# Another order for the instructions of a two-layer convolution and MLP kernel, with some loads issued earlier

## The chip, the cores and the metric

The kernel runs on one core of a Trainium2 chip. The core has five engines with their own instruction streams: TensorE (PE, matrix products into PSUM), VectorE (DVE), ScalarE (ACT), GpSimd (POOL) and SyncE (SP), which here only issues DMAs. The metric is the device time of one execution in microseconds; less is better.

## The reference

One sequence of S = 2048 positions and D = 512 channels passes twice through a pair of layers, in bfloat16. Layer A convolves k with four taps per channel, multiplies by v, convolves the product causally over the whole sequence with a filter of length 2048 per channel (by FFT of length 4096), adds a skip, and multiplies by the layer norm of x. Layer B is an MLP with 1376 hidden features behind two layer norms. Both are added to x.

```python
def _A_ref(q, k, v, shift_k, ssm_k, ssm_D):
    ...
    for t in range(ks):
        k_shift = k_shift + k_pad[:, t:t + S, :] * shift_k[:, ks - 1 - t][None, None, :]
    kv = k_shift * v
    ...
    y_f = kv_f * kf_f[None, :, :, :]
    ...
    y = y + kv * ssm_D[None, None, :]
    return q * y

def _B_ref(x, w1, b1, w2, b2):
    y = _layernorm(x, axis=-1)
    h = _gelu(jnp.einsum("bsd,df->bsf", y, w1) + b1)
    return jnp.einsum("bsf,fd->bsd", h, w2) + b2

x = A_q
x = x + _A_ref(_layernorm(x, axis=-1), A_k, A_v, A_shift_k, A_ssm_k, A_ssm_D)
x = x + _B_ref(_layernorm(x, axis=-1), B_w1, B_b1, B_w2, B_b2)
x = x + _A_ref(_layernorm(x, axis=-1), A_k, A_v, A_shift_k, A_ssm_k, A_ssm_D)
x = x + _B_ref(_layernorm(x, axis=-1), B_w1, B_b1, B_w2, B_b2)
```

Both layers A use the same k, v and filters, so the long convolution y is computed once and used twice.

## The kernel before

**Stages.** The sequence is cut into two halves of 1024 positions. A number at the end of a stage's name is the half. The long convolution is done with matrix products in place of an FFT:

- ht: the filter is transposed on PE (`turn`, L561) and evicted from PSUM to SBUF (L480 on ACT, L481 on DVE).
- fir: k is transposed (L610), the four taps are applied as matmuls (L635 in half 0, L663 in half 1), and DVE multiplies by v while it reads PSUM (L641, L672).
- h1 and x1 (`stage1`, L578): the first transform of the filter and of k·v, eight groups of 16 matmuls in each half, each group evicted as one tile of 128 x 1024.
- h2 and x2 (`stage2`, L590): the second transform, eight groups each. For h2_0 a `swap` follows: eight DMAs of 256 KB on SP's queue (L460, `ar<-ar`) that exchange the partitions of real and imaginary parts.
- Products with the swapped spectrum on DVE (L475): sixteen of 128 x 1024 in half 0; in half 1 eight large ones called p2 (128 x 2048), eight after x2_1, and eight sums, all 128 x 2048.
- i1 and i2: the inverse transforms (L695, L717).

Then come the token blocks, 13 of them, q0 to q12: half 0 takes the 8 tiles of 128 positions of each layer pair as blocks of 1, 1, 2, 2, 2 tiles and then 2, 2, 2, 2; half 1 as 4, 4 and 4, 4. A block does:

- statistics of x on DVE: L831 (BN_STATS) and L832 (BN_AGGR);
- three small steps from variance to scale and mean: L836, L838 (a power with exponent -0.5, always on POOL), and the scaled mean, one instruction on DVE (L843) or one for each tile on POOL (L846);
- the norm, on ACT (L856) or DVE (L857), times y plus x (L475, 128 x 512);
- the same statistics again for layer B (called z), its norm, and a transpose by DMA on SP (L900; for the first tiles on PE, L908);
- m1: 11 groups of matmuls with w1 (L920), each followed by the gelu on ACT (L925);
- m2: matmuls with w2 (L954), added to x on DVE (L958), and the store.

Blocks of half 0 run beside the transforms of half 1. Later, when the transforms are done, what is left is mostly m1 and m2.

**What sets the order.** The class `Prog` records 1187 operations, with the memory that each reads and writes. `arrange` then puts them in the order of a table of numbers, `SEQ`; each engine runs its own operations in that order. A second table, `ENGS`, is a string with one letter for each operation that may run on more than one engine (a: ACT, v: DVE, p: POOL), and a third, `BANKS`, gives each PSUM tile its bank. `sync` puts in the semaphore waits that this order needs. Nothing is reordered at run time: an engine whose next instruction waits, waits with all that is behind it. POOL waits for its own last instruction as well.

Loads of 256 KB and more are `paced`: one may not start before the one 99 places ahead of it has landed.

The main lines are these:

```python
self.seq = [self.ops[i] for i in self.SEQ]
...
o.eng = o.engs[0] if len(o.engs) == 1 else {"a": ACT, "v": DVE, "p": POOL}[next(choice)]
...
P.op((DVE, POOL), lambda e: e.tensor_scalar(v, v, m1, a1, ALU.mult, ALU.add), {DVE: 65.0, POOL: 195.0}, reads=[v], writes=[v])
P.op(POOL, lambda e: e.tensor_tensor(r, v, hf, ALU.pow), 420.0 + 149.0 * n, reads=[v, hf], writes=[r])
```

The numbers in such calls are the planner's costs in nanoseconds. With the order given by a table they have no effect on which instruction stands where.

Of the kernel before, what the change touches and what calls it, by code (L numbers as in the profile page):

```python
# [36 lines left out]
class Prog:  # L37
# [65 lines left out]
            "avvvvaappavvapvavavpvvava")  # L103
    BANKS = (
            "26624320240260660466027405640260464422140204626240406006442460424046462022442640460444626002206020640220"
            "04023022660051677767117660640311026376367637332542537030213654742352762454741476061377362300423726574027"
            "07315704314621527766215047034261015330227471565340011503350731745320154030276054756")

    def __init__(self, nc):
# [885 lines left out]
```

## Time and profile before

| | |
|---|---|
| median of 3 runs | 236.0 us (235.88 to 236.41) |
| the profiled execution | 235.91 us |
| its span in the trace | 234.0 us |
| granted clock of PE | 1.00 |
| PE busy | 222.7 us (95%) |
| DVE busy | 178.7 us (76%) |
| ACT busy | 164.5 us (70%) |
| POOL busy | 55.5 us (24%) |

All times are microseconds from the start of the span. A line of the timeline gives start, duration, engine, source line, operation, output tile and input tile with their sizes, the count of like instructions that follow each other, and in square brackets the idle time ahead of them with what ended it. `ar` is the one large SBUF tensor that holds everything in bfloat16, `sm` the small fp32 one for statistics, `ps` is PSUM. Neighbouring instructions overlap by about 0.1 us, so the distance of two starts is somewhat less than the duration shown. In the chain of waits a line gives start, duration, engine, tile and source line; "issue" is time in which the engine waited for nothing that the trace shows.

### The profile page before, as it was taken

To read this page: it belongs to the slowest core of one execution; us is meant where nothing else is said; L and a number is where in the kernel's file an instruction comes from. 1 tells how busy PE (TensorE), PEld (TensorE's weight loads), DVE (VectorE), ACT (ScalarE), POOL (GpSimd) and SP (SyncE) were. 2 spreads that over 40 slices of the span, in tenths; PEclk is the share of its full clock that TensorE was granted. 3 is DMA by queue.
4 is the path that set the end of the run, shared out by engine and by line. 5 is a ranking of instruction groups with operands and counts; after the bars stand their busy time and mean duration, and the time that the engine had idled before them with its cause. 6 is when DMAs were issued, how large, how long until landed. Compare 5 with 4: busy or idle time off the path is not lost.

```text
span 234.0 us, 6498 instructions
## 1 busy us (share of the span) xinstructions
PE 222.7 (95%) x2743; PEld 147.1 (63%) x2765; DVE 178.7 (76%) x362; ACT 164.5 (70%) x262; POOL 55.5 (24%) x113
## 2 busy tenths in 40 slices
PE   7989887999999999999999999999999999999995
PEld 3878776967868596677966576644444444444454
DVE  0699998999999999999999988781777569410222
ACT  2789999989968688999879986488058216802710
POOL 2270132006403405639303331204011120200000
PEclk9999999999999999999999999999999999999999
DMA  6999489928994360033500313401300130170202
GB/s 185 381 386 305 147 229 274 324 65 150 144 211 126 70 158 3 1 48 72 155 4 3 90 24 68 134 3 22 69 0 3 28 62 0 23 115 0 90 0 92
DMA packets 40106, 24.93 MB, mean 107 GB/s; under 512 B 23591, under 2 KB 33677, under 8 KB 40077
## 3 DMA queue, kind: packets, MB, share of 16 engines
q1 hardware_dynamic: 39778, 24.36, 39.7%
q8 instruction: 22, 0.36, 0.7%
q10 hardware_dynamic: 298, 0.16, 0.4%
q14 instruction: 8, 0.06, 0.1%
HBM read 13.23 MB, written 2.10 MB: 66 GB/s over the span
## 4 chain that ended last, share of the span: by engine, by line
PE 58%; DVE 24%; ACT 10%; issue 2%; POOL 2%; DMA 2%; SPq 0%; DVEq 0%
PE ps L920 23%; PE ps L954 23%; DVE ar L475 13%; ACT ar L480 9%; PE ps L695 4%; DVE sm L831 3%; PE ps L590 2%; DMA ar<-in_A_ssm_k_dram 2%; DVE ar L672 2%; DVE ar L958 2%; DVE ar L641 2%; PE ps L717 1%; POOL sm L836 1%; PE ps L578 1%; PE ps L635 1%
## 5 line engine op out<-in xcount | busy, mean ns | idle before, releaser
L925 ACT ACTIVATE ar<-ps,sm 128x256 bf16<-128x256 f32 (+5 forms) x143 | 65.7, 523 | 33.2 <-PE ps L920 32.9
L920 PE MATMUL ps<-ar 128*128 128x256 bf16 (+5 forms) x569 | 81.9, 297 | 0.4 <-ACT ar L480 0.2
L480 ACT ACTIVATE ar<-ps 128x1024 bf16<-128x1024 f32 (+3 forms) x77 | 71.1, 998 | 11.0 <-PE ps L578 3.4
L954 PE MATMUL ps<-ar 128*128 128x512 bf16 (+1 forms) x323 | 75.9, 379 | 1.5 <-issue 0.6
L920 PEld LDWEIGHTS ps<-ar 128*128 128x128 bf16 (+1 forms) x572 | 52.9, 100 | 27.5 <-ACT ar L480 1.1
L475 DVE TENSOR_TENSOR ar<-ar 128x512 bf16<-128x512 bf16 (+2 forms) x104 | 62.7, 646 | 1.5 <-ACT ar L480 0.8
L954 PEld LDWEIGHTS ps<-ar 128*128 128x128 bf16 (+1 forms) x341 | 32.4, 98 | 35.3 <-ACT ar L925 0.4
L958 DVE TENSOR_TENSOR ar<-ar,ps 128x512 bf16<-128x512 bf16 x31 | 20.8, 680 | 32.9 <-PE ps L954 32.9
L831 DVE BATCH_NORM_STATS2 sm<-ar 128x6 f32<-128x512 bf16 x64 | 42.5, 685 | 0.5
L856 ACT ACTIVATE ar<-ar,sm 128x512 bf16<-128x512 bf16 x39 | 30.6, 813 | 12.9 <-DVE sm L843 8.8
L836 POOL TENSOR_SCALAR sm<-sm 128x2 f32<-128x2 f32 (+2 forms) x22 | 9.9, 449 | 89.0 <-DVE sm L832 88.8
L838 POOL TENSOR_TENSOR sm<-sm 128x2 f32<-128x2 f32 (+2 forms) x26 | 21.7, 834 | 25.1 <-DVE sm L836 23.1
L590 PE MATMUL ps<-ar 128*128 128x64 bf16 x512 | 18.4, 193 | 1.5 <-DVE ar L481 0.7
L578 PE MATMUL ps<-ar 128*64 128x128 bf16 x512 | 17.9, 221 | 1.8 <-ACT ar L480 1.2
L590 PEld LDWEIGHTS ps<-ar 128*128 128x128 bf16 x512 | 16.8, 98 | 3.6 <-DVE ar L481 1.3
L578 PEld LDWEIGHTS ps<-ar 128*64 128x64 bf16 x512 | 14.9, 110 | 4.8 <-ACT ar L480 1.9
L481 DVE CAST ar<-ps 128x1024 bf16<-128x1024 f32 x12 | 14.6, 1218 | 1.2 <-PE ps L578 0.9
L846 POOL TENSOR_SCALAR sm<-sm 128x1 f32<-128x1 f32 x34 | 15.1, 460 | 1.6
L695 PE MATMUL ps<-ar 64*128 64x64 bf16 (+1 forms) x384 | 12.4, 203 | 1.0 <-DVE ar L475 0.9
L695 PEld LDWEIGHTS ps<-ar 64*128 64x128 bf16 (+1 forms) x384 | 11.8, 113 | 2.2 <-DVE ar L475 1.0
L857 DVE TENSOR_SCALAR ar<-ar,sm 128x512 bf16<-128x512 bf16 x25 | 10.3, 415 | 2.7 <-POOL sm L846 2.5
L788 DVE SCALAR_TENSOR_TENSOR ar<-ar,sm,ps 128x512 bf16<-128x512 bf16 x16 | 11.1, 740 | 0.3 <-PE ps L590 0.3
(45 smaller groups left out, 93.5 us busy)
## 6 DMA issues: line engine op xcount, KB each, us to landing
ar<-ar SPq DMA_DIRECT2D x16, 256.0 KB, 4.0
ar<-tab_s SPq DMA_DIRECT2D x9, 256.0 KB, 6.3
ar<-in_A_ssm_k_dram SPq DMA_DIRECT2D x8, 256.0 KB, 5.9
ar<-in_A_q_dram SPq DMA_DIRECT2D x8, 256.0 KB, 4.4
ar<-in_A_v_dram SPq DMA_DIRECT2D x8, 256.0 KB, 5.0
out_dram<-ar SPq DMA_DIRECT2D x7, 256.0 KB, 2.5
ar<-in_B_w_dram SPq DMA_DIRECT2D x4, 344.0 KB, 5.2
ar<-in_B_w_dram SPq DMA_DIRECT2D x5, 256.0 KB, 5.2
```

What stands on the lines that cost most here:

```text
L475: return P.op(eng, lambda e: e.tensor_tensor(o, a, b, op), dur, reads=[a, b] + list(more), writes=[o])
L480: return e.activation(dst, src(), AF.Copy)
L578: r = e.matmul(Q(tl, 64 * ri, 64, i * 128, [1, 128]), w, m, start=True, stop=True)
L590: r = e.matmul(Q(tl, 0, 128, i // 8 * 512 + i % 8 * 4, [32, 16], [1, 4]), w, m, start=True, stop=True)
L695: r = e.matmul(Q(tl, 0, 128, i, *([32, 16], [1, 4]) if split else ([1, 128],)), w, m, start=n == 0, stop=n == 1)
L831: P.op(DVE, lambda e, sj=sj, x=x: e.bn_stats(sj, x), 600.0, reads=[x], writes=[sj])
L838: P.op(POOL, lambda e: e.tensor_tensor(r, v, hf, ALU.pow), 420.0 + 149.0 * n, reads=[v, hf], writes=[r])
L856: return e.activation(o, x, AF.Identity, bias=u, scale=r)
L920: r = e.matmul(Q(tl, 0, rows, 0, [1, w]), a, m, start=dk == 0, stop=dk == 3)
L925: P.op(ACT, lambda e, dst=dst, tl=tl, rows=rows, bias=bias, w=w: e.activation(dst, Q(tl, 0, rows, 0, [1, w]), AF.Gelu_apprx_tanh, bias=bia ...
L954: r = e.matmul(Q(tl, 0, 128, 0, [1, 512]), ins[fc][0], ins[fc][1], start=fc == 0, stop=fc == 10)
L958: P.op(DVE, lambda e, x=x, tl=tl: e.tensor_tensor(x, x, Q(tl, 0, 128, 0, [1, 512]), ALU.add), 604.0, reads=[x], writes=[x], tile=tl)
```

## The change

Only the three tables change; the operations are the same 1187. The first 330 entries of `SEQ` come in another order, with loads of weights and of q at other places among them, and the rest is ordered anew. 40 operations run on another engine than before: 19 norms (eleven from ACT to DVE, eight from DVE to ACT), seven PSUM evictions, and otherwise small ones. ACT has 263 operations in place of 266, DVE 364 in place of 362, POOL 92 in place of 91; PE and SP have as many as before.

```diff
     SEQ = (
-        0, 46, 8, 45, 35, 2, 6, 3, 5, 36, 12, 9, 1, 10, 11, 25, 4, 44, 217, 7, 56, 197, 15, 50, 16, 57, 14, 13, 47,
...
+        2, 8, 45, 35, 0, 6, 36, 43, 3, 5, 44, 11, 9, 1, 10, 12, 4, 7, 25, 56, 197, 46, 216, 217, 15, 50, 57, 13, 16,
...
```

What the table moves is seen in the rows of each engine. A row is a source line, the operation, its output tile and input tile or the output's shape, and how many follow each other.

The first place is PE in the prologue, where the second transform of the filter (L590, h2_0) meets the first transform of k·v (L578, x1_0):

```order
 L590 MATMUL ps<-ar 128x16x4 x32
-L578 MATMUL ps<-ar 64x128 x32
-L590 MATMUL ps<-ar 128x16x4 x16
-L578 MATMUL ps<-ar 64x128 x32
-L590 MATMUL ps<-ar 128x16x4 x16
-L578 MATMUL ps<-ar 64x128 x16
+L578 MATMUL ps<-ar 64x128 x16
+L590 MATMUL ps<-ar 128x16x4 x16
+L578 MATMUL ps<-ar 64x128 x32
+L590 MATMUL ps<-ar 128x16x4 x16
+L578 MATMUL ps<-ar 64x128 x32
```

Each group of 16 is one tile. The two h2_0 groups now come after one and three groups of x1_0, where they came after two and four. SP, at the same stage, issues the eight swap DMAs (`ar<-ar`) with these loads between and behind them:

```order
 L460 DMA ar<-ar 64x8x256 x4
 L460 DMA ar<-in_B_w_dram 128x2x512
-L460 DMA ar<-ar 64x8x256 x4
+L460 DMA ar<-ar 64x8x256 x2
+L460 DMA ar<-in_B_w_dram 128x1376
+L460 DMA ar<-ar 64x8x256 x2
+L460 DMA ar<-in_B_w_dram 128x1376
+L460 DMA ar<-in_B_b_dram 128x10x1
+L460 DMA ar<-in_B_w_dram 128x1376
```

A piece of w1 (128x1376) stands between the last two pairs of swaps; another piece of w1 that stood ahead of the swaps is now behind them. Not shown: a piece of w2 (128x2x512) with the bias b2 has come from behind the swaps to ahead of the first.

The second place is ACT around x1_1, the first transform of half 1 (L480, 128x1024), and block q6, whose two norms are L856. Before:

```order
L480 ACTIVATE ar<-ps 128x1024 x2
L925 ACTIVATE ar<-ps,sm 128x256 x2
L480 ACTIVATE ar<-ps 128x1024
L925 ACTIVATE ar<-ps,sm 128x256
L480 ACTIVATE ar<-ps 128x1024
L856 ACTIVATE ar<-ar,sm 128x512
L480 ACTIVATE ar<-ps 128x1024 x3
L925 ACTIVATE ar<-ps,sm 128x256
L856 ACTIVATE ar<-ar,sm 128x512
```

And of the change:

```order
L480 ACTIVATE ar<-ps 128x1024 x2
L856 ACTIVATE ar<-ar,sm 128x512
L925 ACTIVATE ar<-ps,sm 128x256
L856 ACTIVATE ar<-ar,sm 128x512
L480 ACTIVATE ar<-ps 128x1024 x3
L925 ACTIVATE ar<-ps,sm 128x256
L480 ACTIVATE ar<-ps 128x1024 x2
L856 ACTIVATE ar<-ar,sm 128x512
L925 ACTIVATE ar<-ps,sm 128x256
```

Before, one norm of q6 (the first L856) stands behind four evictions; the other is on DVE. Now both are on ACT and stand behind two evictions. The last L856 of each piece belongs to the z statistic of block q5.

The third place is DVE around the last aggregate (L832) of q6, among the p2 products (L475, 128x32x64, the 128 x 2048 ones of the trace). Before, where the second L832 is that of q6:

```order
L475 TENSOR_TENSOR ar<-ar 128x32x64
L832 BN_AGGR sm<-sm 128x2
L475 TENSOR_TENSOR ar<-ar 128x32x64
L831 BN_STATS sm<-ar 128x6
L475 TENSOR_TENSOR ar<-ar 128x512
L832 BN_AGGR sm<-sm 128x2
L475 TENSOR_TENSOR ar<-ar 128x32x64 x3
L958 TENSOR_TENSOR ar<-ar,ps 128x512
L475 TENSOR_TENSOR ar<-ar 128x32x64
```

And of the change, where the first L832 is that of q6:

```order
L475 TENSOR_TENSOR ar<-ar 128x32x64
L832 BN_AGGR sm<-sm 128x2
L475 TENSOR_TENSOR ar<-ar 128x32x64
L475 TENSOR_TENSOR ar<-ar 128x512
L475 TENSOR_TENSOR ar<-ar 128x32x64
L831 BN_STATS sm<-ar 128x6
L475 TENSOR_TENSOR ar<-ar 128x32x64 x3
L831 BN_STATS sm<-ar 128x6
```

The aggregate has moved up: five large products are behind it now where four were.

More of the change, by code (lines that the diff above doesn't have):

```diff
@@ L44 @@
     SEQ = (
[55 rows of a table removed]
[55 rows of a table added]
     ENGS = (
-            "pvavvvvvavpvpapapaaavaaaaavaavaavavvvppvvvaavvaaavaavvaaaaaaaaavaaaaavaaaavaaaaaaapppvaaaaaaaaaaaaaaaaaa"
-            "avaaaaaaaaapvapvvavpvppaappvvpvaavpaappaappaappaappaappavppvappaappaappvappaapvaapvavvavvvvvapvvvvvppvaa"
-            "avvvvaappavvapvavavpvvava")
+            "pvaavvvvaapvvapvpaaaaaavvavaavaavavvvppvpvaavvaaavaavvaaaaaaaaavaaaaavaaaavaaaaaaavpppaaaaaaaaaaaaaaaava"
+            "aaaaaaaaaaappvpvvappvppaappvvpvaappaappaappaappaappaappvappaappvappaappavppaappaapvavavvvvvavpvvvavpvaaa"
+            "apvvvvavvvvvvvvaavvpvvvva")
     BANKS = (
-            "26624320240260660466027405640260464422140204626240406006442460424046462022442640460444626002206020640220"
-            "04023022660051677767117660640311026376367637332542537030213654742352762454741476061377362300423726574027"
-            "07315704314621527766215047034261015330227471565340011503350731745320154030276054756")
+            "06644620240260460466027405640260460422120204620426406026440246202657402442442202402046620620262446022424"
+            "40045202760061271673611270720311476106045110176745457463524552047013405341600727657677006645241006432235"
+            "02011725663061347154745325226234547674263125476530423505220630623103453761310741074")
     def __init__(self, nc):
```

108 rows, old and new, of the table SEQ are left out of this document.

## Prediction, made before the changed kernel ran

> **What bounds the kernel now.** I read the page first for which engine is full in which slice, then windows by stage, then the chain of waits, then each engine's timeline where the chain changes hands.
>
> ```profile
> span 234.0 us, 6498 instructions
> PE   7989887999999999999999999999999999999995
> DVE  0699998999999999999999988781777569410222
> ```
>
> TensorE (PE) is full from about slice 9 (53 us) to the end; VectorE (DVE) is full from slice 3 to slice 22 (129 us). The profiled execution took 235.91 us, of which the span is 234.0; the median of the runs is 236.0, 0.1 above it. I sum against 235.91. The windows below give, after the bounds and the length of a stretch, the busy time of PE, PE's weight loads, DVE, ScalarE (ACT) and GpSimd (POOL), then clock, DMA share and GB/s.
>
> ```profile
> 6.50:41.30 34.80, 30.04 (x765) 26.48 (x764) 31.75 (x52) 31.90 (x35) 9.69 (x24) 1.00 0.89 285
> 41.30:70.00 28.70, 27.74 (x491) 22.10 (x498) 27.99 (x58) 25.30 (x47) 6.89 (x17) 1.00 0.82 178
> 70.00:121.00 51.00, 50.26 (x688) 37.95 (x681) 50.42 (x83) 45.44 (x83) 20.58 (x28) 1.00 0.30 74
> 130.50:231.70 101.20, 100.69 (x525) 51.52 (x532) 58.82 (x147) 51.74 (x89) 13.57 (x25) 1.00 0.20 46
> ```
>
> PE is idle for 4.8 us before 41.3, then 1.0, 0.7 and, over the last 101 us, 0.5. The clock is 1.00 everywhere. So two things can move the end: when PE's full stretch begins, and any new hole in it. The chain of waits (start, us, engine, output tile, line) shows the hand-overs:
>
> ```profile
> 27.26 1.10 issue
> 41.32 7.39 PE ps L695 x128
> ...
> 90.35 3.35 POOL sm L836
> 93.70 0.07 issue
> 93.77 0.71 POOL sm L838
> 94.49 0.09 issue
> 94.58 1.17 POOL sm L846 x2
> 95.77 0.81 ACT ar L856
> ...
> 108.48 12.51 DVE ar L475 x11
> ```
>
> The first hand-over is in the prologue: the chain goes from the last eviction of h2_0 through the swaps to inverse1 of half 0 (L695, 41.32). The second, at 90 us, is a statistic of block q6: three small POOL steps that here take 5.2 us, then the norm on ACT (L856). The third is DVE's run of products that releases inverse1 of half 1. PE's last matmul ends at 231.7, and what follows it (the last add and store, and what lies outside the span) is 4.2 us of the 235.91. None of those operations changes.
>
> **The prologue: the swaps go out sooner.** The instruction counts hardly move (40 operations change engine, none is added), so the terms are waits and order.
>
> ```profile
> 8.59 1.23 DVE L481 CAST ar<-ps 128x1024 bf16<-128x1024 f32 x1 [0.33 <-PE ps L578]
> 21.36 1.22 DVE L481 CAST ar<-ps 128x1024 bf16<-128x1024 f32 x1
> 24.92 1.21 DVE L481 CAST ar<-ps 128x1024 bf16<-128x1024 f32 x1
> 26.05 0.68 DVE L831 BATCH_NORM_STATS2 sm<-ar 128x6 f32<-128x512 bf16 x1
> 27.22 1.23 DVE L481 CAST ar<-ps 128x1024 bf16<-128x1024 f32 x1 [0.33 <-PE ps L590]
> ```
>
> The CAST at 27.22 is the last eviction of h2_0; the swaps' DMAs wait for it. In the new order two things happen on the way. From 8.59 to the first x1_0 CAST at 21.36 DVE has 11.9 us of work and 0.9 of waiting. Its new list there starts at about 8.14 (before the printed wait of 0.33 and what is left of the instruction ahead; an estimate) with a small product, has one CAST more (1.13, the distance from 24.92 to 26.05), a norm and a halo copy more, and a mask product and some small work less: net +0.66. With the waiting gone, that CAST comes at 8.14 + 12.56 = 20.7, 0.66 sooner. Then PE takes each of the last two h2_0 groups one x1_0 group sooner, so the CAST of h2_0 no longer waits for PE. Between the two CASTs lie 5.86 us before (0.33 of which is the printed wait, and 0.25 another one); the new list has the same four CASTs, one more AGGR of 0.1, and no reason for either wait: 4.8 to 5.3. The CAST moves from 27.22 to 25.5, by 1.7; with the upper figure by 1.2.
>
> ```profile
> 28.48 3.28 SPq L460 DMA_DIRECT2D ar<-ar  x4
> 31.80 0.64 SPq L460 DMA_DIRECT2D ar<-in_B_w_dram  x1
> 33.25 3.21 SPq L460 DMA_DIRECT2D ar<-ar  x4
> DMA to landing us min/median/max: 2.9/4.8/5.6
> 36.35 6.11 DVE L475 TENSOR_TENSOR ar<-ar 128x1024 bf16<-128x1024 bf16 x10 [0.82 <-ACT ar L480]
> ```
>
> SP issues eight swaps in two fours, from 28.48 and from 33.25, each about 0.8 apart and landing after 4.8 (median). DVE's products follow, and the first i1_0 matmul at 41.32 follows them. Moving the first four by 1.7 gives 26.8; the second four depend on later evictions and move by 1.3, to 31.95. A w1 piece of 344 KB now stands between the last two pairs on the queue; at the window's 285 GB/s it is 1.2 us of DMA time, and 0.8 of issue time by the spacing of the swaps. The products wait for swaps pairwise and DVE works through them without a gap, so I take it as mostly hidden: i1_0 starts at 39.8 in place of 41.32, **−1.5**. Bounds: −1.7 (all of the CAST) and −0.3 (the w1 piece delays the last pair by its whole 1.2).
>
> **The loads that go sooner.** The first w2 piece moves from the middle of the program to before the first swap; w1 pieces move a few places, three queries one or two. No wait on a load ends last before 60 us in the chain, other than ssm_k's at the very start, so sooner landings win nothing by themselves: 0. Their cost is the queue time above, in the range 0 to 1.2.
>
> **Carrying −1.5 forward.** DVE is full between 41 and 121 (78.4 busy of 79.7), so it stays 1.5 earlier, and PE with it, until something with its own clock comes. That is the q6 statistic.
>
> **The new wait at q6.** Its last aggregate and what follows it on each engine, before:
>
> ```profile
> 90.06 0.19 DVE L832 BATCH_NORM_AGGREGATE sm<-sm 128x2 f32<-128x6 f32 x1
> 90.16 3.48 DVE L475 TENSOR_TENSOR ar<-ar 128x2048 bf16<-128x2048 bf16 x3
> 90.49 1.94 ACT L480 ACTIVATE ar<-ps 128x1024 bf16<-128x1024 f32 x2 [0.63 <-PE ps L578]
> 97.81 0.50 POOL L846 TENSOR_SCALAR sm<-sm 128x1 f32<-128x1 f32 x2
> 96.49 2.83 ACT L480 ACTIVATE ar<-ps 128x1024 bf16<-128x1024 f32 x3
> 99.20 0.48 ACT L925 ACTIVATE ar<-ps,sm 128x256 bf16<-128x256 f32 x1
> 99.45 0.63 PE L590 MATMUL ps<-ar 128*128 128x64 bf16 x16
> 100.78 0.19 POOL L836 TENSOR_SCALAR sm<-sm 128x2 f32<-128x2 f32 x1 [2.48 <-DVE sm L832]
> 105.67 1.13 POOL L836 TENSOR_SCALAR sm<-sm 128x2 f32<-128x2 f32 x1 [2.75 <-DVE sm L832]
> 105.52 2.36 DVE L475 TENSOR_TENSOR ar<-ar 128x2048 bf16<-128x2048 bf16 x2
> 108.54 4.54 POOL L846 TENSOR_SCALAR sm<-sm 128x1 f32<-128x1 f32 x2
> 108.41 5.77 DVE L475 TENSOR_TENSOR ar<-ar 128x2048 bf16<-128x2048 bf16 x5
> ```
>
> POOL's L836 takes 0.19 at 100.78, where DVE runs statistics, but 3.34 at 90.35, until the third of three 128x2048 products is over (the chain's 3.35), and 1.13 beside the products at 105.52. The two L846 at 108.54 take 2.27 each, two products each. So beside a run of large products a POOL step here lasts one to three of them.
>
> After, the aggregate stands earlier in DVE's list: after 1.5 of upstream gain and 1.7 of DVE work that now lies behind it, it comes at 86.85. Behind it stand a large product, a small one, a large one (together 2.65, so to 89.6), one statistic of 0.6, three large products (to 93.6), one statistic. POOL's L836 waits out the first group and ends about 89.7; L838 (0.71) fits into the statistic and ends about 90.5; the two L846 meet the run of three. At 2.27 each they would outlast it, so they end with it: the means are ready at **X = 93.5**. Before, they were ready at 95.75.
>
> That is sooner, and yet worse, since ACT's order changed more. Before, both x1_1 evictions of 90.49, two more and three gelus stood ahead of the first L856, and the second norm of q6 was on DVE. After, both norms of q6 are on ACT, and only two evictions stand ahead of them. ACT is through with these at about 90.3 (92.4, where the pair above ends, less the 1.5 and less the 0.63 that it waited; an estimate) and then waits for X: 3.2 us. Behind the first norm (0.72 from its start at 95.77 to the next at 96.49) wait a gelu that a w2 group on PE needs (0.38 of the 0.48 above, the rest overlaps), the second norm, five more evictions of x1_1 (0.91 each by the three at 96.49) and one more gelu: 0.72 + 0.38 + 0.72 + 4.55 + 0.38 = 6.75 from X to the first L590 matmul of half 1, which needs all of x1_1: **100.25**, where before it is at 99.45. PE, which the upstream gain had brought 1.5 ahead, is idle for 0.8 + 1.5 = 2.3 us on the way, first ahead of the w2 group that the gelu feeds.
>
> **The sum.** From the first x2_1 group PE is full to its end: 231.67 − 99.45 = 132.2 before. I take the same after, since 100.7 of the last 101.2 us are matmuls that both have. 93.5 + 6.75 + 132.2 = 232.45, against 231.67: +0.8. So 235.91 + 0.8 = **236.7 us**. Moved work in the last 100 us (eleven norms from ACT to DVE, eight the other way, two means from DVE to POOL) lies beside PE with DVE 58% and ACT 51% busy; I put it at 0, with 0.4 either way for one late norm.
>
> **Rivals.**
>
> *The POOL steps are held by one product each.* The rows for it: 1.13 at 105.67 for one L836, though a second product came right behind. Against it: 3.34 at 90.35 and 2.27 twice at 108.54. Then L838 ends at 90.5, L846 twice at the ends of two products, 91.5 and 92.5: X = 92.5, the first x2_1 group at 99.25, PE's end at 231.45, time **235.7**. The Trainium skill, page "SBUF — State Buffer", section "Who interferes with whom", says that a VectorE instruction with two SBUF inputs holds the port it shares with GpSimd for the whole instruction and that whoever issues first gets it; read literally, POOL gets in when the running product ends. The 3.34 us at 90.35 speaks against that reading, the 1.13 at 105.67 for it.
>
> *POOL is through before the run of three, and the gain of the prologue survives (the other side).* Place: the statistic of 0.6 between the two groups of products, and the change from one product to the next. If L836 starts before the first large product (0.1 us after the aggregate, where at 90.35 it came 0.19 after the product's start), or L838 and both L846 get in around the statistic, then X is 91.3 or less. The point from which it decides is X = 91.3: there the first x2_1 group comes at 91.3 + 6.75 = 98.05, which is 1.4 before 99.45, and with the 1.5 of the prologue it can hardly come sooner. From there each us of X costs one us; below, the gain is kept: 235.91 − 1.4 = **234.5**. For it: with DVE idle or on statistics the three steps take 0.19, 0.71 and 0.25 twice, 1.3 together, and would end at 88.5. Against it: no POOL step in the rows above that began beside a large product ended before that product.
>
> *The swaps are not sooner.* The w1 piece between the last two pairs and the early w2 piece ahead of the first share 285 GB/s with the loads that run there; the DMA share is 0.89 in this window. If the last pair lands 1.2 us later than I have it, i1_0 starts at 41.0, q6 and X move by 1.2 too: 236.7 + 1.2 = **237.9**. For it: the 0.89. Against: swaps land 2.9 to 5.6 after issue with a w2 load already between the fours.
>
> That the change doesn't do what it says, that is, that the sooner loads move nothing, is part of all cases: no case gains by them.
>
> **How the numbers follow.** A difference of 0.2%, 0.47 us, is about what a measurement of this kernel can tell from no change; so same is 235.5 to 236.5. Forecast (own range 236.0 to 237.5): 0.44, of which 0.10 falls within 0.2% and 0.34 is slower. One product each (235.2 to 236.2): 0.20, of which 0.13 is same and 0.07 faster. Kept gain (234.1 to 235.3): 0.23, faster. Swaps not sooner (237.3 to 238.5): 0.13, slower but for 0.01. Faster 0.30, same 0.24, slower 0.46. The range leaves out the lower edge of the kept gain and the upper half of the last case: 234.3 to 238.0.
>
> **What would show it.** In the changed kernel: the last h2_0 CAST at 25.5 and the first i1_0 matmul at 39.8 (right) or after 41 (third rival). POOL's L846 of q6 ending at about 93.5, at 92.5, or before 91.3. ACT idle 3 us before an L856 near 90, released by POOL, and PE idle about 2.3 us in all around an L954 near 92, or neither. The first L590 of half 1 at 100.25. PE's end 132 us after it; if that distance differs by over 0.5, the tail's moved norms matter and my zero for them is wrong.

## The result, and the profile after

The changed kernel takes **238.43 us** (median of ten runs, 236.92 to 239.40) beside 236.22 for the kernel before on the same chip (ten runs, 235.45 to 236.76): a ratio of 1.0089, 95% interval 1.0062 to 1.0115. It is slower by 2.2 us by the medians and 2.1 by the ratio, where +0.8 was forecast; the time lies 0.4 above the range. The profiled execution took 239.05 us. Medians here count every run; a ratio leaves out the runs that took over 1.5% longer than the fastest of their kernel.

The prologue first. In the timeline of the changed kernel (columns as before), SP's queue with the swaps (`ar<-ar`), then DVE from the first CAST of x1_0 to the products, then PE:

```profile
29.95 2.77 SPq L460 DMA_DIRECT2D ar<-ar  x4
32.76 0.84 SPq L460 DMA_DIRECT2D ar<-in_B_w_dram  x1
35.40 1.28 SPq L460 DMA_DIRECT2D ar<-ar  x2
36.72 1.27 SPq L460 DMA_DIRECT2D ar<-in_B_w_dram  x1
38.03 1.28 SPq L460 DMA_DIRECT2D ar<-ar  x2
...
22.62 1.22 DVE L481 CAST ar<-ps 128x1024 bf16<-128x1024 f32 x1
28.70 1.22 DVE L481 CAST ar<-ps 128x1024 bf16<-128x1024 f32 x1 [0.17 <-PE ps L590]
44.10 3.70 DVE L475 TENSOR_TENSOR ar<-ar 128x1024 bf16<-128x1024 bf16 x6 [1.40 <-DMA ar<-ar]
...
23.88 1.09 PE L590 MATMUL ps<-ar 128*128 128x64 bf16 x32 [0.80 <-ACT ar L480]
42.82 3.79 PE L695 MATMUL ps<-ar 128*128 128x128 bf16 x64 [0.25 <-DVE ar L475]
47.95 3.74 PE L695 MATMUL ps<-ar 128*128 128x128 bf16 x64 [1.33 <-DVE ar L475]
```

The swaps go out 1.5 us later than before (29.95 for 28.48), not sooner; in three more executions of this kernel (k1 to k3 below) they begin at 28.38, 28.39 and 29.02. The last pair stands behind a w1 piece whose issue alone takes 1.27, and DVE, which never waited for a swap before, waits 1.40 for it. So i1_0 starts at 42.82 (before 41.32) and then breaks in two: its second half begins at 47.95, behind a hole of 1.33.

Now q6, on POOL and ACT, and the first x2_1 groups on PE:

```profile
91.20 1.07 POOL L836 TENSOR_SCALAR sm<-sm 128x2 f32<-128x2 f32 x1 [6.71 <-DVE sm L832]
93.22 0.83 POOL L846 TENSOR_SCALAR sm<-sm 128x1 f32<-128x1 f32 x2
93.18 1.94 ACT L480 ACTIVATE ar<-ps 128x1024 bf16<-128x1024 f32 x2
94.99 0.83 ACT L856 ACTIVATE ar<-ar,sm 128x512 bf16<-128x512 bf16 x1
102.13 1.61 PE L590 MATMUL ps<-ar 128*128 128x64 bf16 x48
```

The means are ready at 94.05 (93.22 + 0.83), and ACT reaches the norm only at 94.99, with no idle time in its row: in this execution the forecast wait is not there. So the loss of this run must lie ahead of 90 us. To see that in all runs, I cut the time at three marks: the start of the last i1_0 matmul, the first inverse1 matmul of half 1 (L695, called i1_1 below) and the end of PE's last matmul. The three lower rows are the same changed kernel profiled again (experiments k1 to k3).

| execution | us | i1_0 starts | last i1_0 | from there to i1_1 | i1_1 to PE's end | behind it |
|---|---|---|---|---|---|---|
| before | 235.91 | 41.32 | 48.48 | 72.96 | 110.23 | 4.24 |
| changed | 239.05 | 42.82 | 51.47 | 73.06 | 110.36 | 4.16 |
| k1 | 238.14 | 41.96 | 50.53 | 73.07 | 110.38 | 4.16 |
| k2 | 242.63 | 41.26 | 50.04 | 76.96 | 111.46 | 4.17 |
| k3 | 240.01 | 42.58 | 51.12 | 73.05 | 110.38 | 5.46 |

Three losses can be read off. The **prologue** is later by 1.6 to 3.0 us in all four. The **rest** takes the same time as before to 0.3 us, but in k2 it takes 4.0 more in the stretch with q6 and 1.2 more in the last one. And in k3 1.3 us come outside the span (240.01 − 236.9 = 3.1, otherwise 1.8), for a reason that no run shows. Without a wait in the rest the parts add up to 237.6 us where the last i1_0 matmul comes at 50.04 and to 239.1 where it comes at 51.47; by this estimate the prologue alone accounts for the median of 238.43, and seven of the ten timed runs lie between the two.

### The profile page after: what moved, and what is told of

Read it like the earlier page. It is cut to its first block, busy times and chain, and to the rows that moved or that the text cites. A ratio compares the mean times of both kernels' runs of the same rounds, so it can differ in the third digit from the quotient of the medians.

```text
span 237.3 us, 6490 instructions
## 1 busy us (share of the span) xinstructions
PE 224.4 (95%) x2742; PEld 148.1 (62%) x2765; DVE 180.8 (76%) x364; ACT 162.5 (69%) x259; POOL 48.5 (20%) x109
## 4 chain that ended last, share of the span: by engine, by line
PE 81%; ACT 6%; DMA 4%; DVE 3%; issue 2%; SPq 1%; POOL 1%; ACTq 0%; POOLq 0%
PE ps L920 32%; PE ps L954 31%; ACT ar L480 6%; PE ps L578 5%; PE ps L590 4%; PE ps L717 3%; DMA ar<-ar 2%; DMA ar<-tab_small 2%; PE ps L695 2%; PE ps L561 2%; DVE ar L475 1%; SPq L460 1%; PE ps L943 1%; POOL ar L548 1%; PE ps L663 1%
## 5 line engine op out<-in xcount | busy, mean ns | idle before, releaser
L480 ACT ACTIVATE ar<-ps 128x1024 bf16<-128x1024 f32 (+3 forms) x76 | 70.2, 1002 | 13.2 <-PE ps L561 5.2
L475 DVE TENSOR_TENSOR ar<-ar 128x512 bf16<-128x512 bf16 (+3 forms) x105 | 63.0, 636 | 2.4 <-DMA ar<-ar 1.4
L856 ACT ACTIVATE ar<-ar,sm 128x512 bf16<-128x512 bf16 x36 | 28.3, 814 | 2.7 <-POOL sm L846 1.7
L836 POOL TENSOR_SCALAR sm<-sm 128x2 f32<-128x2 f32 (+2 forms) x23 | 6.7, 290 | 96.0 <-DVE sm L832 95.6
L838 POOL TENSOR_TENSOR sm<-sm 128x2 f32<-128x2 f32 (+2 forms) x26 | 20.4, 784 | 25.5 <-DVE sm L836 23.6
L578 PE MATMUL ps<-ar 128*64 128x128 bf16 x512 | 19.4, 231 | 1.4 <-ACT ar L480 0.9
L590 PE MATMUL ps<-ar 128*128 128x64 bf16 x512 | 18.6, 194 | 1.7 <-ACT ar L480 1.6
L590 PEld LDWEIGHTS ps<-ar 128*128 128x128 bf16 x512 | 16.9, 98 | 3.7 <-ACT ar L480 1.5
L578 PEld LDWEIGHTS ps<-ar 128*64 128x64 bf16 x512 | 16.3, 117 | 4.5 <-ACT ar L480 1.9
L481 DVE CAST ar<-ps 128x1024 bf16<-128x1024 f32 x13 | 15.8, 1221 | 3.6 <-PE ps L578 2.3
L695 PE MATMUL ps<-ar 64*128 64x64 bf16 (+1 forms) x384 | 12.5, 203 | 1.7 <-DVE ar L475 1.6
L695 PEld LDWEIGHTS ps<-ar 64*128 64x128 bf16 (+1 forms) x384 | 11.9, 114 | 3.0 <-ACT ar L480 2.2
L846 POOL TENSOR_SCALAR sm<-sm 128x1 f32<-128x1 f32 x29 | 12.4, 442 | 1.6
L832 DVE BATCH_NORM_AGGREGATE sm<-sm 128x2 f32<-128x6 f32 x64 | 10.6, 173 | 0.7
```

What stands on the lines that cost most here:

```text
L475: return P.op(eng, lambda e: e.tensor_tensor(o, a, b, op), dur, reads=[a, b] + list(more), writes=[o])
L480: return e.activation(dst, src(), AF.Copy)
L578: r = e.matmul(Q(tl, 64 * ri, 64, i * 128, [1, 128]), w, m, start=True, stop=True)
L590: r = e.matmul(Q(tl, 0, 128, i // 8 * 512 + i % 8 * 4, [32, 16], [1, 4]), w, m, start=True, stop=True)
L695: r = e.matmul(Q(tl, 0, 128, i, *([32, 16], [1, 4]) if split else ([1, 128],)), w, m, start=n == 0, stop=n == 1)
L856: return e.activation(o, x, AF.Identity, bias=u, scale=r)
```

## Experiments

Ratios are to the kernel before on the same chip, with 95% intervals; 0.001 of a ratio is 0.24 us.

**Which half of the table costs.** d1 has the first 280 operations of the old order, with their engines and banks, and the rest of the new; d2 the reverse.

```diff
 d1: SEQ = old[:280] + new order of the other operations
 d2: SEQ = new[:280] + old order of the other operations
```

> The first 280 operations (up to about 50 us) as in the kernel before, the rest in the order, on the engines and in the banks of the changed kernel. Theories Loads and Compute: nothing is lost behind the prologue, 236.0 to 236.5, and from the end of i1_0 to the start of i1_1 there are 73.0 us as in both kernels. Theory q6: the rest of the order costs what I predicted for it without the gain of the prologue, 2.3 us: 238.0 to 238.5, and the stretch grows to 75.

> The first 280 operations as in the changed kernel, the rest as in the kernel before. Theories Loads and Compute: the whole loss stays, 237.8 to 238.8. Theory q6: 235 to 236.5, for the prologue alone would not lose.

d1: 237.06 us, ratio 1.0019 (0.9996 to 1.0043). d2: 237.51 us, 1.0058 (1.0037 to 1.0078). By the ratios the new prologue costs 1.4 us alone and the new rest 0.45, with an interval that reaches below 0; together 1.8 of the 2.1. d1's runs go from 235.60 to 242.62, and the slowest, the profiled one, has a hole of 2.17 us on PE at 97 us.

**The loads.** c1 is the changed kernel with the loads up to the last swap at their old places in the DMA queues, here shown around the swaps; c2 is the kernel before with the loads up to the last swap at their new places. The loads behind the swaps stay where each kernel has them.

```diff
 c1, SP around the swaps:
 L460 DMA ar<-ar 64x8x256 x4
 L460 DMA ar<-in_B_w_dram 128x2x512
-L460 DMA ar<-ar 64x8x256 x2
-L460 DMA ar<-in_B_w_dram 128x1376
-L460 DMA ar<-ar 64x8x256 x2
+L460 DMA ar<-ar 64x8x256 x4
 and ACT's first two:
-L460 DMA ar<-in_A_ssm_D_dram 1x512
 L470 DMA ar<-tab_small 128x464
+L460 DMA ar<-in_A_ssm_D_dram 1x512
```

> The changed kernel, but the loads up to the last swap are issued in the order of the kernel before (on SP and on ACT); all other orders are the changed kernel's, the order of the eight swaps too. Theory Loads (the order of the loads makes nearly the whole loss: table second, more bytes queued ahead of PE's instruction fetch near 20 us, w1 between the swaps): the stall of PE of 0.8 us ahead of the first h2_0 group and the hole of 1.3 us among the i1_0 groups are gone, i1_0 starts at 40 to 41, time 235.6 to 236.6. Theory Compute (the new order and engines of the prologue's evictions and products make it): still 237.5 to 238.2. Theory q6 (the wait that I predicted, worth 2.3 us in all): at least 236.7.

> The kernel before with the changed kernel's order of loads up to the last swap (the swaps among themselves in the old order). Theory Loads: 237.5 to 238.5, with PE stalled ahead of the first h2_0 group and the last swap landing after 42. Theory Compute: 236.2 to 236.8.

c2: 237.22 us, 1.0040 (1.0021 to 1.0060): the new places of the loads cost 0.95 even under the old order, and in its profile i1_0 starts at 42.06 and DVE waits 0.80 for a swap. c1: 238.49 us, 1.0083 (1.0055 to 1.0112), no better than the changed kernel, although its profile (236.02) has the last i1_0 matmul at 48.40. Its runs fall apart into 236.02, 237.1 and four of 238.4 to 238.7. In the profiled one the loss of the prologue is gone, and yet most are longer. What the loads do to PE is seen in the timelines at the first h2_0 groups and the last h2_0 CAST, of the changed kernel in the execution k1:

```profile
22.31 1.09 PE L590 MATMUL ps<-ar 128*128 128x64 bf16 x32 [0.82 <-ACT ar L480]
27.13 1.22 DVE L481 CAST ar<-ps 128x1024 bf16<-128x1024 f32 x1 [0.17 <-PE ps L590]
```

And of c1:

```profile
21.50 1.35 PE L590 MATMUL ps<-ar 128*128 128x64 bf16 x32
21.11 1.22 DVE L481 CAST ar<-ps 128x1024 bf16<-128x1024 f32 x1
26.34 1.23 DVE L481 CAST ar<-ps 128x1024 bf16<-128x1024 f32 x1 [0.17 <-PE ps L590]
```

With the new loads PE is idle for 0.82 ahead of the group, with the old ones not at all, and the last h2_0 CAST follows, 27.13 against 26.34. The hole, 0.52 to 0.84, stands at this group in eight profiles with the new order and the new loads (the changed kernel, k1 to k3, a1, a3, d2, h1; in a2 a hole of 0.84 stands one group earlier) and in none of six with the new order and the old loads (c1 twice, e2, e3, e4, h2). The eviction that this group waits for had ended 0.9 to 1.2 us sooner. What keeps an even distance to it is a packet of 16 KB on the instruction queue: in the eight profiles PE goes on 1.28 to 1.41 us after that packet is in, wherever it lies between 20.9 and 22.5 us. The Trainium skill, page "Runtime: NRT & Kernel Launch", section "Instruction fetch mechanics", says that an engine's sequencer streams its program in blocks of 16 KiB over a DMA queue of its own, at a cost that is "mostly hidden". Here it would be in view. That the block is the cause is argued and not shown: no run changed it alone, and the trace does not tell whose program a packet carries. Of the six profiles without a hole five fit as well (the group starts 1.37 us or more behind the packet), while in e4 it starts 1.08 behind it; and b1 below, with the old order, has a hole of 0.47 at its first h2_0 group, 1.58 behind the packet. Nor are the DMA engines fuller with the new loads: their share from 19 to 21 us is 1.06 in k1 and 1.00 in c1, though they move 386 GB/s in k1 and 218 in c1.

**PE's start.** The changed table also swaps ACT's first two DMAs, so that the first table lands later (5.17 for 3.87). a1 puts it first again, a2 bridges the wait with nine warm-up matmuls in place of seven, b1 puts it second in the kernel before.

```diff
 a1, ACT:
+L470 DMA ar<-tab_small 128x464
 L460 DMA ar<-in_A_ssm_D_dram 1x512
-L470 DMA ar<-tab_small 128x464
 a2, PE:
-        for i in range(7):
+        for i in range(9):
```

> The changed kernel with one edit: ACT issues the load of the small table (identity and first transform) ahead of the load of the skip vector, as the kernel before does. Theory C (PE's clock): in the changed kernel PE stands idle 0.8 us between its warm-up matmuls and the first transposes, because the table lands later, and works at half its rate until 10.9 us. With the table first, the first transposes come at about 4.6, the first h1_0 groups follow each other by about 0.46 us (0.86 in the changed kernel), the transposes of k (L610) start by 10.3 us in place of 11.77, and the time is 1.2 to 2.0 us shorter: 236.4 to 237.2. Theory L (the load is merely late): everything starts 0.6 us sooner and the time is 0.6 us shorter, 237.8, with the groups still 0.86 apart. Theory W (the w1 load among the swaps makes the loss): the time stays within 0.4 us of 238.4.

> The changed kernel with nine warm-up matmuls in place of seven, so that PE is busy until the table has landed; the loads stay as they are in the changed kernel. Theory C: the first transposes start no sooner than now (5.2 us or a little later), and yet the h1_0 groups come 0.46 us apart from the first or second on, L610 starts by 10.6 us, and the time is about 1.0 to 1.5 us shorter: 237.0 to 237.4. Theory L: nothing is gained, or 0.1 us is lost by the two matmuls: 238.4 to 238.6.

> The kernel before with one edit: ACT issues the skip vector's load ahead of the small table's, as the changed kernel does. Theory C: the table lands about 0.6 us later, PE idles between the warm-up and the transposes, the h1_0 groups come 0.86 us apart, and the time grows by 1.2 to 2.0 us: 237.4 to 238.2. Theory L: plus 0.6 us, 236.8. If the order of these two loads doesn't matter: 236.2.

a1: 238.14 us, 1.0103 (1.0073 to 1.0133); a2: 238.70 us, 1.0107 (1.0089 to 1.0124); b1: 236.63 us, 1.0030 (1.0009 to 1.0051). The place of the table costs the old order 0.7 by the ratio, but curing it does not cure the changed kernel: in a1 the first turn of k (L610) is at 9.78 (before 9.89, in the changed kernel 11.77 and, in k1 to k3, 10.03 to 10.44), and the last swap still lands at 42.6. A miss for the theory that the start carries the loss. e2 gives c1 the old engines and banks of the first evictions:

```diff
-L480 ACTIVATE ar<-ps 128x1024 x3
+L480 ACTIVATE ar<-ps 128x1024 x4
```

> The changed kernel with the old order of loads, and with the first evictions as in the kernel before (one of the first three filter transposes on ACT, the last two on DVE, one skip addition on POOL in place of DVE, two h1_0 evictions exchanged) and the banks of the first PSUM tiles as there, so that PE's third transpose doesn't wait for the eviction of the first. Theory Start (the long runs are those in which PE idles early and its rate doubles late): no run above 237.5 but for one in ten, median 236.0 to 236.6. Theory Swap: still most runs above 238.

239.87 us, 1.0102 (1.0058 to 1.0146): refuted as well.

**What stands between the swaps.** a3 is the changed kernel with the w1 piece behind the last swap. e3 is c1 with the w2 piece behind all eight; e4 is e3 with e2's edit.

```diff
 a3:
 L460 DMA ar<-ar 64x8x256 x2
-L460 DMA ar<-in_B_w_dram 128x1376
 L460 DMA ar<-ar 64x8x256 x2
+L460 DMA ar<-in_B_w_dram 128x1376
 e3:
-L460 DMA ar<-ar 64x8x256 x4
-L460 DMA ar<-in_B_w_dram 128x2x512
-L460 DMA ar<-ar 64x8x256 x4
+L460 DMA ar<-ar 64x8x256 x8
+L460 DMA ar<-in_B_w_dram 128x2x512
```

> The changed kernel with the w1 load that stands between the last two pairs of swaps issued behind the last swap. Theory W: the last swap is issued about 1.3 us sooner and lands before DVE needs it, the hole of 1.33 us between the fourth and the fifth group of inverse1 goes, and the time is about 1.3 us shorter: 237.1. Theory C alone: the swaps land sooner but later waits take the gain; within 0.4 us of 238.4.

> The changed kernel with the old order of loads, and with the w2 piece that stands between the two fours of swaps issued behind the last swap. Theory Swap (i1_0 ends 7.4 us after the last swap lands): the last swap lands about 0.7 us sooner after the first is issued, the hole of 0.85 us in i1_0 goes, and fastest and median run are each 0.5 to 0.8 us below those of the kernel with the old loads (236.0 and 238.5). If the late landing doesn't set the end: no change.

> Both edits together. If both theories hold: median 235.3 to 236.0, below the kernel before (236.2 to 236.4). If only Start holds: 236.0 to 236.6; if only Swap holds: about 237.8.

a3: 237.70 us, 1.0067 (1.0041 to 1.0093), 0.5 better than the changed kernel by the ratios, whose intervals overlap; DVE's wait for a swap falls from 1.40 to 0.48. e3 removes it. Its swaps, DVE's products and i1_0:

```profile
28.18 8.12 SPq L460 DMA_DIRECT2D ar<-ar  x8
36.04 8.52 DVE L475 TENSOR_TENSOR ar<-ar 128x1024 bf16<-128x1024 bf16 x14
41.05 7.41 PE L695 MATMUL ps<-ar 128*128 128x128 bf16 x128 [0.25 <-DVE ar L475]
```

No gap is left: fourteen products in one run, i1_0 in one piece, its last matmul at 48.24, even 0.24 ahead of the kernel before. So in this execution the late prologue is undone by the loads alone. But the time is not: e3 takes 239.73 us, 1.0107 (1.0060 to 1.0153), with runs from 236.85 to 242.12, and e4 238.89, 1.0102 (1.0066 to 1.0138). In their profiles both lose it behind i1_0: e3 has the wait at q6 that k2 shows below (ACT 2.98, PE 2.17), e4 the one at the z statistic (PE 0.99). What the other runs lose it to is not shown.

**The two waits in the rest.** k1 to k3 profile the changed kernel itself again.

> The changed kernel as it is, profiled anew, to see which of its losses return in another execution. Theory prologue (fixed in the order): the first batch of h2_0's half (i1_0) ends at 50.2 to 51.5 us again, against 48.48 before. Theory chance (GpSimd beside VectorE's products): the stretch from the end of i1_0 to the start of i1_1 is 73.0 us without a hole at 95 us and 76 to 77 with one; the stretch from there to TensorE's end 110.3 or 111.5. If the 236.9 to 239.4 us of the timed runs comes from these two places, each profiled time is 4.15 us plus the sum of the three stretches, within 0.3.

> The same kernel a second time: the same three stretches. If theory prologue holds, i1_0's end differs from the other profile by under 0.7 us; if theory chance holds, L836 of q6's norm is again 1.07 or 2.54 us, with a hole of 2.2 us on TensorE only in the long case.

> The same kernel a third time, with the same expectations: the end of i1_0 at 50.2 to 51.5 us, and the two GpSimd places short or long independently of it.

The table above holds them: the prologue was late each time, though not by one fixed amount (50.04 to 51.12, and 51.47 in the first profile, where 50.2 to 51.5 and at most 0.7 between two executions were expected), and k2 has both waits. Its q6, on POOL, ACT and PE, and then the z statistic of block q8, on ACT and PE:

```profile
89.76 2.54 POOL L836 TENSOR_SCALAR sm<-sm 128x2 f32<-128x2 f32 x1 [6.70 <-DVE sm L832]
93.19 3.42 POOL L846 TENSOR_SCALAR sm<-sm 128x1 f32<-128x1 f32 x2
96.65 0.81 ACT L856 ACTIVATE ar<-ar,sm 128x512 bf16<-128x512 bf16 x1 [2.96 <-POOL sm L846]
98.26 3.19 PE L954 MATMUL ps<-ar 128*128 128x512 bf16 x7 [2.53 <-ACT ar L925]
...
143.72 0.81 ACT L856 ACTIVATE ar<-ar,sm 128x512 bf16<-128x512 bf16 x1 [1.00 <-POOL sm L846]
144.95 1.05 PE L920 MATMUL ps<-ar 128*128 128x256 bf16 x8 [0.99 <-ACT ar L925]
```

The order of the instructions is the same as in k1, where the four POOL steps of q6 take 2.9 us together; here they take 6.9, and ACT and PE wait behind them. The seven matmuls behind the hole take 3.19 in place of 1.67 in the other executions; the granted clock is 0.74 from 95 to 101 us. Short or long is decided anew in each execution. At the z statistic c1 shows both, in two executions of one kernel:

```profile
135.29 1.22 POOL L846 TENSOR_SCALAR sm<-sm 128x1 f32<-128x1 f32 x2
135.38 2.43 DVE L475 TENSOR_TENSOR ar<-ar 128x512 bf16<-128x512 bf16 x7
```

```profile
136.18 2.89 POOL L846 TENSOR_SCALAR sm<-sm 128x1 f32<-128x1 f32 x2
136.27 2.43 DVE L475 TENSOR_TENSOR ar<-ar 128x512 bf16<-128x512 bf16 x7
```

In both, POOL's two steps start 0.09 us ahead of seven small products on DVE; once they are through after 1.22, once they last as long as the whole run of products. The second execution has the hole of 0.99 on PE and took 238.15, where the first took 236.02; another 0.9 of the difference lies ahead of it, for the last i1_0 matmul comes at 49.30 in place of 48.40. The second is c1 run again:

> The changed kernel with the old order of loads once more, for a second profile: its six runs lay at 236.0, 237.1 and four times 238.4 to 238.7, and the profile was of the 236.0. Theory Start: a run at 238.4 or more shows PE at half rate until 10 us or later and the transposes of k (L610) after 11.5 (9.86 in the profile at 236.0). Theory Swap: L610 is near 10 and the last swap lands after 43 (41.0 in the profile at 236.0). A run near 236 again tells nothing.

h1 and h2 take these steps off POOL: q6's L836 and its means, and the mean of the z statistic, are done by DVE; h1 in the changed kernel, h2 in e3.

```diff
 h1, DVE around q6:
 L832 BN_AGGR sm<-sm 128x2
+L836 TENSOR_SCALAR sm<-sm 128x2
 L475 TENSOR_TENSOR ar<-ar 128x32x64
 L475 TENSOR_TENSOR ar<-ar 128x512
 L475 TENSOR_TENSOR ar<-ar 128x32x64
 L831 BN_STATS sm<-ar 128x6
-L475 TENSOR_TENSOR ar<-ar 128x32x64 x3
+L475 TENSOR_TENSOR ar<-ar 128x32x64
+L843 SCALAR_TENSOR_TENSOR sm<-sm 128x2
+L475 TENSOR_TENSOR ar<-ar 128x32x64 x2
```

> The changed kernel with three small statistic steps moved from POOL to DVE: the first and the third of q6, and the scaled mean of z8; the power stays on POOL. Theory Lottery (POOL steps beside DVE's products last one of two lengths by chance, and the long one costs 2.9 us at q6 and 1.25 at z8): the runs come closer together, none shows a PE hole near 95 or 139, and the median falls from 238.4 to 236.9 to 237.6; what is left is the prologue. Theory Swap alone (the prologue makes the loss): the median stays within 0.4 us of 238.4.

> The changed kernel with the old order of loads, the w2 piece behind the last swap, and the three steps off POOL. If both theories hold: i1_0 ends at 48.2 or sooner, 73 us to the second inverse, median 235.4 to 236.2, that is 0.1 to 0.9 below the kernel before. If the lottery goes on at other POOL steps: some runs at 237 and more.

Neither comes near the kernel before. h1: 239.85 us (239.27 to 239.97), 1.0139 (1.0118 to 1.0159), slower than the changed kernel (1.0089); h2: 238.10 us, 1.0068 (1.0043 to 1.0092), 0.9 us better than e3 by ratios whose intervals overlap. The long wait is gone from both profiles, but the mean on DVE now stands behind three large products, a small one and a statistic, and ACT waits for it in both (here h1):

```profile
94.41 0.15 DVE L843 SCALAR_TENSOR_TENSOR sm<-sm 128x2 f32<-128x2 f32 x1
94.59 0.81 ACT L856 ACTIVATE ar<-ar,sm 128x512 bf16<-128x512 bf16 x1 [0.74 <-DVE sm L843]
```

From the last i1_0 matmul to i1_1 both take 0.8 more than before (73.74 and 73.77 for 72.96), where the four profiles of the changed kernel have 0.1 or 4.0. h1 adds to that a late prologue (50.21) and stores that end 1.3 later behind PE, in its profile.

h3 puts both q6 norms on ACT behind two evictions in the kernel before, the placement that the prediction priced.

```diff
 L480 ACTIVATE ar<-ps 128x1024 x2
+L856 ACTIVATE ar<-ar,sm 128x512
+L925 ACTIVATE ar<-ps,sm 128x256
+L856 ACTIVATE ar<-ar,sm 128x512
-L925 ACTIVATE ar<-ps,sm 128x256 x2
+L925 ACTIVATE ar<-ps,sm 128x256
```

> The kernel before with one part of the change: both norms of q6 on ACT and behind two x1_1 evictions, as in the changed kernel; all else as before. Theory Lottery and my forecast of the wait: where POOL's steps end 5.5 us after the aggregate, as in the kernel before, ACT waits 3 us, PE has a hole of 2 to 2.5 us near 93 us, and the time is 2 to 3 us longer: 238.2 to 239.2 in most runs. If the place of the norms on ACT doesn't matter: 236.2.

240.99 us, 1.0181 (1.0140 to 1.0221), the slowest of all. ACT and PE around q6:

```profile
94.38 0.81 ACT L856 ACTIVATE ar<-ar,sm 128x512 bf16<-128x512 bf16 x1 [1.60 <-POOL sm L846]
96.67 0.61 PE L920 MATMUL ps<-ar 128*128 128x256 bf16 x4 [2.94 <-ACT ar L925]
```

From the last i1_0 matmul to i1_1 it takes 77.48, 4.5 more than before. With the old order of all else the placement alone costs that, even in an execution where POOL was quick (L836 in 1.07): ACT waits 1.60 for the means, and PE waits 2.94 for a gelu that stands behind the norms on ACT.

## Why the prediction was wrong

**The bounds** were right: PE's full stretch, once begun, takes as long as before. From the last i1_0 matmul to i1_1 and from there to PE's end the changed kernel takes 73.05 to 73.07 and 110.36 to 110.38 us where no wait hits (before 72.96 and 110.23).

**The step that failed first is the prologue**: "i1_0 starts at 39.8 in place of 41.32, −1.5". It started at 41.26 to 42.82, and its last matmul came 1.6 to 3.0 later than before, where 1.5 sooner was forecast. Three parts of the step fell:

- "no reason for either wait: 4.8 to 5.3" between the first x1_0 CAST and the last h2_0 CAST. With the old loads (c1) it is 5.23 (21.11 to 26.34), as forecast; with the new ones 6.1 (22.62 to 28.70), because PE stops for 0.8 ahead of the first h2_0 group. The loads were to cost nothing but queue time. The first CAST, forecast at 20.7, came at 21.03 in k1 and 21.11 in c1, so even without the hole the gain was 0.9 (c1's swaps at 27.6), not 1.7.
- "mostly hidden" for the w1 piece. It took 1.27 of SP's time in the profiled run (0.62 to 1.97 in k1 to k3) and stood ahead of two swaps; the last one, issued at 38.68, landed at 44.08, after 5.4 us, where before it was issued at 35.77 and landed at 40.22. DVE does not work through its products without a gap; it waits 1.2 to 1.5 for the last swap in all four executions. (The 4.8 that the prediction took for the landing of swaps is the median of a row that counts loads too; the eight swaps before landed after 2.9 to 5.2.)
- The start was not looked at. The swapped DMAs of ACT let PE stop before its first transposes, for 0.58 in the profiled run and 0.35 to 0.45 in k1 to k3. By a1 and a2 this is not what makes the time.

**The third rival** ("the swaps are not sooner", 237.9, chance 0.13) is what happened, and its own range of 237.3 to 238.5 holds the time, but in part by luck: its 237.9 counts the 2.3 of the q6 wait, which most executions do not have. Its mechanism, the w1 piece ahead of the last pair, is one part (without it DVE's wait falls to 0.48 in a3's profile, and a3 is 0.5 better by ratios whose intervals overlap), and its price of 1.2 was too small: against the forecast 39.8 for the start of i1_0 the loss is 1.5 to 3.0, and the hole inside i1_0 comes on top. The range cut this case at 238.0.

**The q6 wait, the second step that failed,** is right as a mechanism and in the length of its waits, too small in its cost (2.3 forecast, 4.0 in k2) and wrong in how often it comes. Forecast: ACT waits 3.2, PE is idle 2.3, POOL is held by one group of three products and then by another. k2 shows 2.96 and 2.53, with POOL held just so, and h3 shows the cost of the placement by itself. But one of the four executions of the changed kernel has it. In the other three L836 is held by one product, as the first rival had it, and the means are ready 3.1 us behind the aggregate (k1: 90.03 to 93.14), before the run of three products, as the second rival had it (X at 91.3 or less, that is 4.5 behind its aggregate at 86.85; the forecast 93.5 is 6.7 behind). ACT then comes later than the means. The ten timed runs lie between 236.92 and 239.40, 2.5 us apart, and the wait costs 4.0, so none of them seems to have it. So q6 does not make the median. That the forecast came within 1.7 us of the time is luck: the prologue was wrong by 3.1 to 4.5 us one way, and the 2.3 of q6, mostly absent, the other way.

The Trainium skill, page "SBUF — State Buffer", section "Who interferes with whom", on which the first rival leaned, has whoever issues first hold the shared port pair for the whole instruction while the other engine fully blocks; it says so of VectorE's 2-port modes, and of an instruction with two SBUF inputs, such as these products, that it contends with a GpSimd instruction that reads SBUF. The short runs agree (L836 in 1.07 beside a product of 1.2). The long ones (2.54 beside two large products and a small one, 2.65 for one L846 beside seven small ones) do not: POOL stays out across several instructions of DVE. What chooses between the two is open; c1's two executions started it at the same distance.

**The tail** was put at 0 ± 0.4. Its order costs 0.15; but one of the two means that went to POOL brings the wait of 1.0 at 145 us in k2 (and in the profiles of c1's second execution, e2 and e4), which was not foreseen. The prediction's own sign for this zero is tripped: from the first x2_1 group to PE's end it takes 132.8 in k1 (before 132.2). But 0.4 of these 0.6 lie ahead of i1_1, where the group comes 0.3 sooner behind i1_0, and not in the tail.

**The sum** by what was measured: prologue +1.4 (d2), rest +0.45 (d1), together 1.8 of 2.1; the 0.3 that is left is within the intervals. What stays open is why curing the prologue does not cure the time: c1, e3, e4 and h2 have the last i1_0 matmul within 0.3 us of the kernel before in a profile, and their medians are 1.7 to 3.6 us above it. No order tried here beats the kernel before.

## What to carry to other kernels

When loads are moved ahead of a transfer on the critical path, count every queue they share with it, the issue time on the queue's engine, and the landing time under load; with a piece between the last two pairs of swaps DVE waited 1.2 to 1.5 us for the last one here, and 0.5 with the piece behind them. An order with a GpSimd step on the path beside back-to-back VectorE products has no one time: profile it several times, and put work of the waiting engine ahead of the wait, so that either outcome is covered. A path that is cured early in a program need not make the program shorter (e3), so measure the parts apart and together.

## What the runs showed of the hardware beyond that

**PE is slow for its first microseconds, and for how long varies.** In the profiled run of the changed kernel, and before:

```profile
8.08 3.76 PE L578 MATMUL ps<-ar 128*64 128x128 bf16 x80
```

The same 80 matmuls took 2.50 before. The starts of its matmuls (of its pairs of matmuls, in this row) are 106.7 ns apart until 10.85 us and 56 after; before, that changed between 6.2 and 6.81, in k1 to k3 at 5.2, 5.8 and 7.5. The profile's row of the granted clock shows nothing of it: 1.00 from 2 to 11 us. At the first h2_0 group the profiled run is 1.57 us behind k1 (23.88 for 22.31), at its last i1_0 matmul 0.9; that the slow start is the reason is likely and was not tested.

**A hole of 2 to 3 us on PE can be followed by slow matmuls.** From 95 to 101 us of k2 the granted clock is 0.74, and 0.97 in the five after that (below, the third number from the end):

```profile
95.00:101.00 6.00, 3.47 (x34) 1.74 (x31) 5.22 (x13) 4.35 (x6) 3.38 (x6) 0.74 0.00 1
101.00:106.00 5.00, 4.95 (x94) 3.66 (x93) 2.00 (x5) 4.23 (x7) 1.24 (x4) 0.97 0.13 26
```

So the forecast idle time of 2.3 cost 4.0: the hole of 2.53, and about 1.5 of matmuls at a lower clock behind it (3.19 − 1.67). It need not be so. In e2 eight matmuls of the same kind take 1.90 right behind a hole of 2.18, and the clock stays at 1.00:

```profile
96.83 1.90 PE L954 MATMUL ps<-ar 128*128 128x512 bf16 x8 [2.18 <-ACT ar L925]
95.00:101.00 6.00, 3.70 (x45) 2.16 (x46) 4.20 (x12) 5.39 (x8) 2.33 (x6) 1.00 0.00 1
```

There the stretch from the last i1_0 matmul to i1_1 takes 75.99, 3.0 more than before, where k2's takes 4.0 more and e3's, with a hole of 2.17 and a clock of 0.72 from 95 to 101 us, 4.2. What decides it is open.
